# Attention with a mixture of experts on one core: row sums completed on VectorE instead of GpSimd, a batch's gating in 22 small steps further apart, another order of work within a pair of heads

## The chip, the cores and the metric

One core of a Trainium2 chip runs the kernel. The metric is the device time of one execution in microseconds. The engines are TensorE (PE in the profile; its weight loads are PEld), VectorE (DVE), ScalarE (ACT), GpSimd (POOL) and SyncE (SP), which issues most DMAs. Each takes its instructions in the order in which the program holds them.

## The reference

Attention over 8 batches, 8 heads, 576 positions and 64 numbers a head, float32, with a threshold: scores that lie more than tau under their row's maximum count as nothing. Its output is the input of a mixture of 8 experts, of which each token takes the two with the highest noisy logit.

```python
scores = scale * np.matmul(q, k.transpose(0, 1, 3, 2))
thresh = np.max(scores, axis=-1, keepdims=True) - tau
scores = np.where(scores >= thresh, scores, -1000000000.0)
attn = np.exp(scores - np.max(scores, axis=-1, keepdims=True))
attn = attn / (np.sum(attn, axis=-1, keepdims=True) + 1e-09)
x = np.matmul(attn, v)            # then (B, S, H * D) -> (4608, 512)
logits = x @ w_gate
noisy_logits = logits + np.log1p(np.exp(x @ w_noise)) * noise
top2 = np.argpartition(-noisy_logits, 2, axis=1)[:, :2]
# top2_w: softmax of the two logits; for each expert e and its tokens:
out[mask] += top2_w[mask, k, None] * (np.maximum(x[mask] @ w1[e], 0.0) @ w2[e])
```

## The kernel before

The program has two stages. In the attention stage, up to about 640 us, the work goes in 32 pairs of heads, n = 0 to 31, four for each batch, in the order of their numbers but overlapped: a pair's score work runs beside the value work of the pair before it.

For a pair, `split` cuts keys and queries into a high part (hik, hiq, on ACT, L199) and the rest (lok, loq, on POOL, L200); the scores are three products of these on PE (`scores`, L240), into two PSUM buffers sp. There are nine row blocks a pair, 0 to 8; block 0 holds the two heads' last 64 rows, 1 to 8 are 128 rows each. For each block VectorE reads sp and takes the row maximum (`rowmax`, L253, called R0 to R8 below), ACT the exponentials e (L255) and the threshold thr (L259), and VectorE masks e by the threshold into p and sums the row (`mask`, L278; M0 to M8). PE transposes p in pieces (`ptile`, L289), ACT copies them to pt (L291), and PE multiplies them with the values (`avpiece`, `avrem`, L343). `pcorner` (L315, L317) and `prem` (L304 to L308) do the same for the last 64 rows and columns. `norm` adds 1e-9 to the row sums on POOL (L328, L329), `invert` takes their reciprocals on VectorE (L334, L335); `oev` copies the product out (L370, ACT), `xlpart` transposes it and multiplies it with the gate's weights (L386, L387), `xev` scales it with the reciprocals (L400, VectorE; X0, X1).

After its fourth pair a batch is gated by ten functions, most of them on POOL, during the following three pairs: sums of the logits (t, lgs), softplus of the noise scale (ab, ge, gln, gu, gr, gc), the two largest of eight (`gate_max`), their one-hot rows (oh), ranks within each expert by a product on PE (`gate_rank`: mb, rk), slots (sl). Then ten scatters, each an indirect DMA that POOL issues (`gate_put`, L617, with a memset of a spacer ahead of it), write the tokens into slot_table, in DRAM.

In the second stage, to the end, the experts run: tokens are read from the table (ti, L809, SP; ix, L819, VectorE), gathered (L839, POOL), multiplied (L893, L914) and added to the output by indirect DMA (L935, POOL). The first expert starts on the tokens of batches 0 to 5 before the attention stage ends.

The order of work on every engine is written out by hand. Each call gets a key, and the calls are issued in the order of their keys:

```python
    for n in range(NP):
        g = 9 * n
        d = dict(PAIR, **(LAST if n == NP - 1 else {}))
...
    for _, _, f, a in sorted(ev, key=lambda x: x[:2]):
        f(*a)
```

So nine units of a key are one pair. `PAIR` holds the offsets of a pair's calls, `LAST` those of the last pair, `GATING` those of a batch's gating behind the last xev of its fourth pair, and `START` those of the first expert, counted from G = 9 x 32.

Of the kernel before, what the change touches and what calls it, by code (L numbers as in the profile page):

```python
# [27 lines left out]
NB = 5  # L28
# [15 lines left out]
    mask=(1.47, 3.69, 4.19, 5.44, 6.30, 7.74, 7.98, 8.87, 9.48),
    ptile=(3.86, 4.04, 7.93, 7.95, 10.00, 8.13, 13.46, 10.48, 12.98), pcorner=(5.79,), prem=(10.10,), norm=(14.32,),
    invert=(14.85,), avrem=(14.96,), avpiece=(11.09, 12.01, 12.31, 14.67, 15.74, 15.85, 16.05, 16.25),
    oev=(16.02, 16.72), xlpart=(16.96, 19.35, 20.02), xev=(18.74, 20.37), split_q=(-7.96,), split_k=(-9.92,))
# [3 lines left out]
    mask=(1.32, 1.83, 4.56, 2.84, 5.96, 6.40, 7.00, 9.93, 10.16),  # L51
    ptile=(4.62, 6.52, 7.86, 5.64, 10.07, 8.69, 9.18, 10.55, 10.85), pcorner=(2.03,), prem=(11.01,), norm=(10.90,),
    invert=(11.92,), avrem=(11.47,), avpiece=(11.27, 11.29, 11.64, 11.68, 11.41, 11.44, 12.80, 12.82),
    oev=(12.91, 13.26), xlpart=(13.13, 13.45, 14.05), xev=(13.15, 14.22))
# [4 lines left out]
GATING = (0, 2, 2.2, 3.5, 5, 7, 8, 10.5, 11.3, 13)  # L59
# [12 lines left out]
    gate=(6, 7, 7, 8, 8, 9, 9, 10, 11, 11), put=(12, 12, 12, 13, 13, 13, 13, 13, 13, 13), tokb=13, ixb=17,  # L72
# [71 lines left out]
def attention(tc, const, work, psum, state, qk, v, tau, wgn, noise, noise_r, out, x_dram, table, experts):  # L144
# [401 lines left out]
    def gate_max(b):  # L546
        d = gt[b]
        d["mx"] = small([NB, 8], F32, "mx")
        d["ix"] = small([NB, 8], U32, "ix")
        for i in range(NB):  # L550
            vec.max(d["mx"][:, i, :], d["nl"][:, i, :])
        for i in range(NB):
            vec.max_index(d["ix"][:, i, :], d["mx"][:, i, :], d["nl"][:, i, :])
# [640 lines left out]
```

## Time and profile before

| what | us |
|---|---|
| median of 3 runs (1490.82 to 1495.47) | 1493.9 |
| the profiled execution | 1491.48 |
| its span | 1489.7 |
| busy: PE, VectorE, ACT, POOL | 1407.6, 875.8, 699.9, 590.0 |

The profile is of one execution, whose mean granted clock of TensorE was 0.975 of full speed. An engine's busy time counts its instructions' durations; what is left of the span it waits. Since each engine goes in order, an instruction that waits holds up all that stand behind it on its engine.

### The profile page before, as it was taken

How to read it: one execution, taken by the hardware profiler on the slowest of the kernel's cores; microseconds unless marked ns; L12 is line 12 of the kernel's file. 1: busy time of each engine (PE TensorE's matmuls, PEld its weight loads, DVE VectorE, ACT ScalarE, POOL GpSimd, SP SyncE). 2: the span in 40 equal slices, each digit the busy share in tenths (PEclk: the TensorE clock that was granted, in tenths of full speed). 3: DMA queues.
4: the chain of work that ended last, by engine and by line, in shares of the span. 5: the costliest groups of instructions: out<-in, count | busy, mean ns of one | idle time of the engine just before them, and what ended most of it. 6: DMA issues, size and time to landing. Idle time of an engine off the chain costs nothing. (4 is left out here: it accounts for less than half of the span.)

```text
span 1489.7 us, 25931 instructions
## 1 busy us (share of the span) xinstructions
PE 1407.6 (94%) x9242; PEld 1200.6 (81%) x9242; DVE 875.8 (59%) x2502; ACT 699.9 (47%) x1447; POOL 590.0 (40%) x785
## 2 busy tenths in 40 slices
PE   8998989899898998898999999999999999999996
PEld 5776767677676776696998998999999999989884
DVE  7887878788787977563554354344454553543411
ACT  6996879788887876540322122122132231221210
POOL 2145454445453545553252252262352432531512
PEclk9999999999999998999999999999999999999998
DMA  5242424233332224255657466376386375563422
GB/s 169 61 132 65 132 65 132 65 111 86 99 91 61 69 60 130 72 146 114 183 125 170 105 147 150 84 160 148 91 183 150 83 183 138 123 165 92 67 28 32
DMA packets 154116, 166.32 MB, mean 112 GB/s; under 512 B 58148, under 2 KB 105340, under 8 KB 152960
## 3 DMA queue, kind: packets, MB, share of 16 engines
q1 hardware_dynamic: 126784, 125.21, 28.9%
q0 software_dynamic: 27200, 39.42, 16.0%
q8 instruction: 73, 1.20, 0.4%
q14 instruction: 59, 0.48, 0.1%
HBM read 104.42 MB, written 60.15 MB: 110 GB/s over the span
## 5 line engine op out<-in xcount | busy, mean ns | idle before, releaser
L255 ACT ACTIVATE e<-ns,nm 128x576 f32<-128x576 f32 x288 | 214.0, 772 | 90.3 <-DVE ns L253 85.9
L253 DVE TENSOR_SCALAR_CACHE_REDUCE ns<-sp 128x576 f32<-128x576 f32 x279 | 203.4, 751 | 37.2 <-PE sp L240 37.2
L278 DVE SCALAR_TENSOR_TENSOR p<-ns,thr,e 128x576 f32<-128x576 f32 x256 | 216.7, 862 | 1.2 <-ACT thr L259 1.2
L240 PE MATMUL sp<-hik,hiq 128*128 128x288 f32 (+1 forms) x558 | 124.8, 350 | 43.0 <-DVE ns L253 41.6
L289 PE MATMUL tp<-ident,p 128*128 128x128 f32 x1024 | 154.9, 289 | 8.0 <-DVE p L278 4.8
L240 PEld LDWEIGHTS sp<-hik,hiq 128*128 128x128 f32 (+1 forms) x558 | 69.5, 188 | 102.4 <-DVE ns L253 67.1
L291 ACT ACTIVATE pt<-tp 128x512 f32<-128x512 f32 x256 | 144.1, 595 | 13.4 <-PE tp L289 10.2
L343 PE MATMUL tp<-pt,vt 128*64 128x256 f32 (+1 forms) x1024 | 148.0, 414 | 0.0
L935 POOL DMA_INDIRECT out<-m_y,ix x54 | 87.8, 1627 | 150.4 <-DVE m_y L974 137.5
L935 POOL DMA_INDIRECT out<-m_y,sx x43 | 67.6, 1572 | 194.6 <-DVE m_y L916 176.0
L289 PEld LDWEIGHTS tp<-ident,p 128*128 128x128 f32 x1024 | 124.7, 152 | 17.9 <-PE tp L289 5.5
L895 ACT ACTIVATE m_p<-m_tp 128x384 fp32r<-128x384 f32 (+1 forms) x66 | 32.6, 494 | 211.8 <-PE m_tp L893 210.1
L916 DVE TENSOR_SCALAR m_y<-m_sp,gw 128x512 f32<-128x512 f32 (+1 forms) x43 | 32.3, 751 | 154.7 <-PE m_sp L914 153.3
L200 POOL TENSOR_TENSOR lok<-kq,hik 128x640 fp32r<-128x640 f32 x31 | 48.3, 1557 | 169.3 <-ACT hik L199 169.3
L240 PE MATMUL sp<-lok,hiq 128*128 128x288 f32 (+1 forms) x558 | 103.8, 301 | 0.0
L343 PEld LDWEIGHTS tp<-pt,vt 128*64 128x64 f32 x1024 | 79.7, 136 | 29.6 <-issue 10.8
L839 POOL DMA_INDIRECT m_p<-x_rows,sx x71 | 69.6, 980 | 81.6 <-DMA stage<-m_p 55.0
L240 PE MATMUL sp<-hik,loq 128*128 128x288 f32 (+1 forms) x558 | 100.3, 294 | 0.0
L617 POOL DMA_INDIRECT slot_table<-pay,sl x80 | 87.0, 1088 | 16.7 <-issue 14.1
L895 ACT ACTIVATE m_hik<-m_tp 128x384 fp32r<-128x384 f32 (+1 forms) x11 | 5.6, 506 | 181.1 <-PE m_tp L893 181.1
L893 PE MATMUL m_tp<-m_pt,m_pt 128*128 128x384 f32 (+1 forms) x396 | 73.3, 343 | 0.0
L893 PE MATMUL m_tp<-m_vt,m_pt 128*128 128x384 f32 (+1 forms) x264 | 71.8, 346 | 0.0
(349 smaller groups left out, 3504.6 us busy)
## 6 DMA issues: line engine op xcount, KB each, us to landing
m_kq<-w SPq DMA_DIRECT2D x128, 256.0 KB
kq<-qk SPq DMA_DIRECT2D x32, 640.0 KB
stage<-m_p SPq DMA_DIRECT2D x63, 256.0 KB
vt<-v SPq DMA_DIRECT2D x8, 1280.0 KB
out<-zeros SPq DMA_DIRECT2D x19, 512.0 KB
x_rows<-xr SPq DMA_DIRECT2D x32, 256.0 KB
...
```

The costliest lines, as they stand in the source:

```text
L200: nc.gpsimd.tensor_tensor(lo, x, hi.bitcast(F32), op=ALU.subtract)
L240: nc.tensor.matmul(sp[s][:, hh, 0:HALF], q_[p, 128 * t:128 * t + 128] if j else q_[:, 512:640], k_[p, k0:k0 + HALF], start=(i == 0), stop= ...
L253: nc.vector.tensor_scalar(ns, sp[:, :, 0:HALF], -1.0 / math.sqrt(D) if n else scale, None, op0=ALU.mult, op1=ALU.min, accum_out=nm)
L255: nc.scalar.activation(e, ns, AF.Exp, bias=nm, scale=-1.0)
L278: nc.vector.scalar_tensor_tensor(p, ns, thr, e, op0=ALU.is_le, op1=ALU.mult, accum_out=ssum[n][:, c:c + 1])
L289: nc.tensor.transpose(tp[:, kt, :], p[:, 128 * kt:128 * kt + 128], ident)
L291: nc.scalar.activation(pt[n][:, s, :, COLS[t]:COLS[t] + 128], tp, AF.Copy)
L343: nc.tensor.matmul(av[n, i][64 * s:64 * s + 64, 0:PIECES[i][1] - PIECES[i][0]], w, x, start=(k == 1), stop=(k == 5))
L617: st = nc.gpsimd.indirect_dma_start(out=table, out_offset=bass.IndirectOffsetOnAxis(ap=d["sl"][0:m, i, c:c + 1], axis=0), in_=d["pay"][0:m ...
L839: self.nc.gpsimd.indirect_dma_start(out=r[0:m], out_offset=None, in_=x, in_offset=bass.IndirectOffsetOnAxis(ap=self.tok[e][2][0:m, t:t + 1 ...
L893: nc.tensor.matmul(ps[:, 0:n], w[:, 128 * c:128 * c + 128], x[:, c, 0:n], start=(i == 0), stop=(i == len(ops) - 1))
L935: st = self.nc.gpsimd.indirect_dma_start(out=out, out_offset=bass.IndirectOffsetOnAxis(ap=idx, axis=0), in_=y, in_offset=None, compute_op= ...
```

## The change

`norm` becomes one addition on VectorE (L327) over the 128x9 block of row sums; the sums of the last rows of the second head, which L328 moved across partitions, are now moved by the reciprocal (L331). The ten gating functions become fourteen: the reciprocal gr, the sum of the one-hot rows and the addition of the base ranks stand by themselves, and the five maxima and the five index searches are issued one by one, at offsets up to 17.8 rather than 13. The scatters follow 18.6 units behind the last xev rather than 14.8, 0.85 apart. The offsets of `PAIR` and `LAST` are other numbers, so are some of `START`. Lines after L253 mostly move by a few: scores L241, row maximum L254, e L256, thr L260, mask L279, splits L200 and L201, scatter L624, ix L828.

```diff
 PAIR = dict(
-    scores=(-1.65, 0.71, 1.60, 3.60, 6.29), rowmax=(-0.38, 1.14, 1.15, 1.78, 1.82, 4.85, 5.21, 6.69, 7.81),
+    scores=(-1.92, -0.37, 3.30, 4.27, 5.98), rowmax=(-1.42, 1.95, 2.09, 3.33, 3.37, 5.08, 5.21, 6.30, 6.64),
...
-GATING = (0, 2, 2.2, 3.5, 5, 7, 8, 10.5, 11.3, 13)
+GATING = (0, 2.2, 2.4, 3.6, 5.2, 5.4, (7.6, 8.1, 8.6, 9.1, 9.6), (10.1, 10.6, 11.1, 11.6, 12.1), 12.7, 13.2, 14.8, 15.6, 16.6, 17.8)
...
-    raw=(-20, -20, -10), tok=-35, ix=-30, ga=(-30, -28, -26), ba=(-28, -26, -24), la=(-26, -22, -20), ta=(-12, -11, -8),
+    raw=(-20, -20, -10), tok=-31, ix=-27, ga=(-27, -25, -23), ba=(-25, -23, -21), la=(-23, -20, -18), ta=(-12, -11, -8),
...
     def norm(n):
 
-        r = ssum.pop(n)
-
-        eng = nc.vector if experts and n >= NP - 2 else nc.gpsimd
-        eng.tensor_scalar(r[0:64, 9:10], r[64:128, 8:9], 1e-9, None, op0=ALU.add)
-        eng.tensor_scalar(r[:, 0:9], r[:, 0:9], 1e-9, None, op0=ALU.add)
-        rn[n] = r
+        r = rn[n] = ssum.pop(n)
+        nc.vector.tensor_scalar(r[:, 0:9], r[:, 0:9], 1e-9, None, op0=ALU.add)
 
     def invert(n):
         r = rn[n]
+        nc.vector.reciprocal(r[0:64, 9:10], r[64:128, 8:9])
         nc.vector.reciprocal(r[:, 0:9], r[:, 0:9])
-        nc.vector.reciprocal(r[0:64, 9:10], r[0:64, 9:10])
...
+    def gate_inverse(b):
+        u, c, r = gt[b]["soft"]
+        vec.reciprocal(r, u)
+
     def gate_soft2(b):
         eng = engine(b)
         d = gt[b]
         l, (u, c, r) = d["l"], d["soft"]
-        vec.reciprocal(r, u)
         eng.tensor_tensor(c, c, r, op=ALU.mult)
...
-            x = g + d["xev"][1]
+            x = g + max(d["xev"])
...
-                to = x + 14.8 + 0.9 * i
+                to = x + 18.6 + 0.85 * i
```

The first place is POOL's row among the scatters of the first batch. Behind "waits" stand semaphores: DMASW belongs to the DMAs that POOL issues, DMAHW to the loads, and each other to an engine. Before:

```order
L616 MEMSET spacer 1x1 [waits Pool_49]
L617 DMA slot_table<-pay_1793,sl_1836 37152x2
L616 MEMSET spacer 1x1 [waits Pool_49]
L617 DMA slot_table<-pay_1793,sl_1836 37152x2
L616 MEMSET spacer 1x1 [waits Pool_49]
L617 DMA slot_table<-pay_1793,sl_1836 37152x2
L328 TENSOR_SCALAR ssum_1673<-ssum_1673 64x1 [waits DMASW4_49,DMASW3_49,DMASW5_49,DMASW2_49,DMASW6_49,DMASW1_49,DMASW0_49]
L329 TENSOR_SCALAR ssum_1673<-ssum_1673 128x9 [waits DVE_49,Pool_49]
L616 MEMSET spacer 1x1
L617 DMA slot_table<-pay_1793,sl_1836 37152x2
L616 MEMSET spacer 1x1 [waits Pool_49]
L617 DMA slot_table<-pay_1793,sl_1836 37152x2
```

Now:

```order
L624 DMA slot_table<-pay_1996,sl_2044 37152x2
L623 MEMSET spacer 1x1 [waits Pool_49]
L624 DMA slot_table<-pay_1996,sl_2044 37152x2
L623 MEMSET spacer 1x1 [waits Pool_49]
L624 DMA slot_table<-pay_1996,sl_2044 37152x2 [waits DMASW0_49]
L201 TENSOR_TENSOR lok_2260<-kq_1783,hik_2259 128x640 [waits Activation_49]
L623 MEMSET spacer 1x1 [waits Pool_49]
L624 DMA slot_table<-pay_1996,sl_2044 37152x2 [waits DMASW1_49]
L201 TENSOR_TENSOR loq_2393<-kq_2072,hiq_2392 128x640 [waits DMAHW3_49,PE_49,Activation_49]
```

L328 and L329 are gone from among the scatters; a scatter now follows the other, with lok between the ninth and the tenth.

The second place is POOL's row in a batch's first gating pair, where xr is the logits, gu, gc and gr belong to the noise scale. Before:

```order
L200 TENSOR_TENSOR loq_1354<-kq_1000,hiq_1353 128x640 [waits PE_49,Activation_49]
L501 TENSOR_TENSOR t_1423<-xr_120 128x320 [waits DVE_49]
L504 TENSOR_TENSOR t_1425<-t_1423 128x160 [waits Pool_49]
L506 TENSOR_TENSOR lgs_1427<-t_1425 128x80 [waits Pool_49]
L328 TENSOR_SCALAR ssum_1133<-ssum_1133 64x1 [waits Pool_49]
L329 TENSOR_SCALAR ssum_1133<-ssum_1133 128x9 [waits Pool_49]
L528 TENSOR_SCALAR gu_1514<-ge_1483 128x40 [waits Activation_49]
L529 TENSOR_SCALAR gc_1515<-gu_1514 128x40 [waits Pool_49]
L530 TENSOR_TENSOR gc_1515<-ge_1483,gc_1515 128x40 [waits Pool_49]
L538 TENSOR_TENSOR gc_1515<-gc_1515,gr_1516 128x40 [waits DVE_49,Pool_49]
```

Now:

```order
L498 TENSOR_TENSOR t_1483<-xr_120 128x320 [waits DVE_49]
L501 TENSOR_TENSOR t_1485<-t_1483 128x160 [waits Pool_49]
L503 TENSOR_TENSOR lgs_1487<-t_1485 128x80 [waits Pool_49]
L201 TENSOR_TENSOR loq_1562<-kq_1250,hiq_1561 128x640 [waits DMAHW7_49,PE_49,Activation_49]
L524 TENSOR_SCALAR gu_1593<-ge_1569 128x40 [waits Activation_49]
L525 TENSOR_SCALAR gc_1594<-gu_1593 128x40 [waits Pool_49]
L526 TENSOR_TENSOR gc_1594<-ge_1569,gc_1594 128x40 [waits Pool_49]
L537 TENSOR_TENSOR gc_1594<-gc_1594,gr_1595 128x40 [waits DVE_49,Pool_49]
L538 TENSOR_TENSOR gc_1594<-gc_1594,gln_1571 128x40 [waits Activation_49,Pool_49]
```

The subtraction loq, ahead of the logits' sums before, now stands between them and gu.

The third place is VectorE's row in the same pair, around the reciprocal gr; p masks of blocks M and pr the mask of block 0 (M0), ns the row maxima. Before:

```order
L334 RECIPROCAL ssum_1133<-ssum_1133 128x9 [waits Pool_49]
L335 RECIPROCAL ssum_1133<-ssum_1133 64x1
L278 SCALAR_TENSOR_TENSOR p,ssum_1381<-ns_1410,thr_1406,e_1412 128x576
L253 TENSOR_SCALAR ns_1535,nm_1536<-sp_1520 128x576 [waits DVE_49,PE_49]
L537 RECIPROCAL gr_1516<-gu_1514 128x40 [waits Pool_49]
L278 SCALAR_TENSOR_TENSOR p,ssum_1381<-ns_1477,thr_1479,e_1481 128x576 [waits Activation_49]
L253 TENSOR_SCALAR ns_1569,nm_1536<-sp_1521 128x576 [waits DVE_49,PE_49]
```

Now:

```order
L254 TENSOR_SCALAR ns_1548,nm_1549<-sp_1534 128x576 [waits DVE_49,PE_49]
L510 SCALAR_TENSOR_TENSOR ab_1567<-lgs_1487 128x40 [waits Pool_49]
L279 SCALAR_TENSOR_TENSOR p,ssum_1354<-ns_1516,thr_1518,e_1520 128x576 [waits Activation_49]
L279 SCALAR_TENSOR_TENSOR p,ssum_1354<-ns_1523,thr_1518,e_1525 128x576
L279 SCALAR_TENSOR_TENSOR p,ssum_1354<-ns_1468,thr_1462,e_1470 128x576
L531 RECIPROCAL gr_1595<-gu_1593 128x40 [waits Pool_49]
L279 SCALAR_TENSOR_TENSOR pr_1626,ssum_1625<-ns_1548,thr_1550,e_1552 128x576 [waits DVE_49,Activation_49]
L254 TENSOR_SCALAR ns_1628,nm_1629<-sp_1576 128x576 [waits DVE_49,PE_49]
```

The reciprocal gr, between a row maximum and a mask before, now follows four masks with a row maximum among them and stands just ahead of M0.

With these tables VectorE's row of a pair without gating reads, after the change: R1 R2 X0 R3 R4 M1 M2 M3 M4 R5 R6 X1, norm and the two reciprocals, R7 R8 M5, R0 of the next pair, M7 M8 M6, M0 of the next pair. On ACT hik stands between the fourth and the fifth e of a row of nine, hiq behind the copies that follow the e of block 0.

## Rows read from the trace of the kernel before

**Rows 1.** The page's part 1, busy time of each engine.
```profile
PE 1407.6 (94%) x9242; PEld 1200.6 (81%) x9242; DVE 875.8 (59%) x2502; ACT 699.9 (47%) x1447; POOL 590.0 (40%) x785
```

**Rows 2.** Windows: a pair without gating, then one batch's first three gating pairs.
```profile
57.99:74.37 16.38, 16.38 (x154) 12.54 (x154) 14.22 (x42) 15.27 (x33) 3.63 (x5) 1.00 0.30 90
...
90.76:107.91 17.15, 17.13 (x158) 13.00 (x156) 14.29 (x42) 15.60 (x35) 10.62 (x16) 1.00 0.75 216
107.91:126.56 18.65, 18.15 (x161) 13.50 (x158) 17.05 (x65) 15.65 (x34) 6.62 (x14) 1.00 0.23 65
126.56:150.79 24.23, 17.57 (x137) 13.82 (x138) 16.54 (x44) 15.24 (x32) 15.66 (x25) 0.88 0.21 50
```

**Rows 3.** Windows 90.76 to 475.91, one for each of five batches: sum line.
```profile
sum 385.15, PE 349.51 PEld 266.47 DVE 308.59 ACT 310.11 POOL 181.88; mean PE 69.90 PEld 53.29 DVE 61.72 ACT 62.02 POOL 36.38
```

**Rows 4.** Windows 475.91 to 589.39; timeline of PE, floor pair's first score matmul.
```profile
568.08:589.39 21.31, 14.24 (x126) 9.81 (x122) 12.85 (x53) 11.98 (x26) 9.56 (x16) 0.90 0.35 104
sum 113.48, PE 101.73 PEld 76.54 DVE 90.56 ACT 89.39 POOL 59.30; mean PE 16.96 PEld 12.76 DVE 15.09 ACT 14.90 POOL 9.88
...
70.95 0.40 PE L240 MATMUL sp<-hik,hiq 128*128 128x288 f32 x1
```

**Rows 5.** Waits between 100 and 600 us: total, times, longest.
```profile
DVE ssum L334 <- POOL ssum L329: 46.7, 7, 7.9
```

**Rows 6.** Timeline of POOL, VectorE and PE in the first stall.
```profile
143.54 0.23 POOL L328 TENSOR_SCALAR ssum<-ssum 64x1 f32<-64x1 f32 x1 [4.28 <-DMA slot_table<-pay,sl]
...
144.15 0.22 DVE L334 RECIPROCAL ssum<-ssum 128x9 f32<-128x9 f32 x1 [6.96 <-POOL ssum L329]
...
145.84 0.61 PE L240 MATMUL sp<-hik,hiq 128*128 128x288 f32 x1 [5.81 <-DVE ns L253]
```

**Rows 7.** Windows after the first stall.
```profile
146.00:150.00 4.00, 4.00 (x20) 3.98 (x21) 4.00 (x11) 3.42 (x8) 2.27 (x5) 0.50 0.03 3
```

**Rows 8.** Timeline: loq on POOL and what VectorE ran beside it; a mask alone.
```profile
60.53 1.61 POOL L200 TENSOR_TENSOR loq<-kq,hiq 128x640 fp32r<-128x640 f32 x1 [0.98 <-ACT hiq L199]
...
61.56 0.76 DVE L253 TENSOR_SCALAR_CACHE_REDUCE ns<-sp 128x576 f32<-128x576 f32 x1 [0.84 <-PE sp L240]
...
66.38 0.81 DVE L278 SCALAR_TENSOR_TENSOR p<-ns,thr,e 128x576 f32<-128x576 f32 x1
...
110.44 1.56 POOL L200 TENSOR_TENSOR loq<-kq,hiq 128x640 fp32r<-128x640 f32 x1 [0.98 <-ACT hiq L199]
...
110.75 1.87 DVE L278 SCALAR_TENSOR_TENSOR pr<-ns,thr,e 128x576 f32<-128x576 f32 x1
```

**Rows 9.** Groups of instructions (page, all, 100 to 600 us); tile ssum's L329.
```profile
L255 ACT ACTIVATE e<-ns,nm 128x576 f32<-128x576 f32 x288 | 214.0, 772 | 90.3 <-DVE ns L253 85.9
L253 DVE TENSOR_SCALAR_CACHE_REDUCE ns<-sp 128x576 f32<-128x576 f32 x279 | 203.4, 751 | 37.2 <-PE sp L240 37.2
L278 DVE SCALAR_TENSOR_TENSOR p<-ns,thr,e 128x576 f32<-128x576 f32 x256 | 216.7, 862 | 1.2 <-ACT thr L259 1.2
...
L291 ACT ACTIVATE pt<-tp 128x512 f32<-128x512 f32 x256 | 144.1, 595 | 13.4 <-PE tp L289 10.2
...
L259 ACT ACTIVATE thr<-nm,atau 128x2 f32<-128x2 f32 (+1 forms) x160 | 45.6, 285 | 0.0
...
L199 ACT ACTIVATE hiq<-kq,some 128x640 fp32r<-128x640 f32 x31 | 25.6, 827 | 0.0
...
L528 POOL TENSOR_SCALAR gu<-ge 128x40 f32<-128x40 f32 x7 | 3.4, 488 | 9.2 <-ACT ge L518 9.2
...
L329 DVE TENSOR_SCALAR ssum<-ssum x2: 173/509/845, 605.8 to 618.0; 128x9 f32<-128x9 f32 x2
```

**Rows 10.** Timeline: last early scatter (POOL), table read (SP), its use (VectorE).
```profile
530.04 1.10 POOL L617 DMA_INDIRECT slot_table<-pay,sl  x1 [0.21 <-issue]
...
533.79 1.72 SPq L809 DMA_DIRECT2D ti<-slot_table  x4
...
546.20 0.24 DVE L819 TENSOR_SCALAR ix<-ti,jq 128x24 int32<-128x24 int32 x1
```

More of the change, by code (lines that the diff above doesn't have):

```diff
@@ L42 @@
 PAIR = dict(
-    scores=(-1.65, 0.71, 1.60, 3.60, 6.29), rowmax=(-0.38, 1.14, 1.15, 1.78, 1.82, 4.85, 5.21, 6.69, 7.81),
[L44 to L47, printed above, removed]
-LAST = dict(
[L51 to L54, printed above, removed]
+    scores=(-1.92, -0.37, 3.30, 4.27, 5.98), rowmax=(-1.42, 1.95, 2.09, 3.33, 3.37, 5.08, 5.21, 6.30, 6.64),
+    mask=(1.85, 3.58, 4.11, 5.05, 5.06, 7.09, 9.10, 8.99, 9.05),
+    ptile=(7.22, 6.78, 10.70, 6.07, 7.59, 12.31, 12.70, 10.22, 10.71), pcorner=(5.58,), prem=(11.03,), norm=(14.52,),
+    invert=(15.23,), avrem=(13.45,), avpiece=(12.87, 13.19, 13.58, 14.04, 13.51, 14.11, 16.71, 17.48),
+    oev=(14.49, 19.23), xlpart=(19.31, 20.92, 22.57), xev=(20.54, 23.30), split_q=(-10.40,), split_k=(-5.20,))
+LAST = dict(
+    scores=(-1.92, -0.37, 2.95, 4.28, 5.25), rowmax=(-1.42, 1.77, 2.48, 2.96, 3.44, 4.42, 4.44, 6.36, 7.05),
+    mask=(1.53, 3.58, 3.71, 5.27, 6.21, 7.13, 7.68, 7.76, 9.27),
+    ptile=(5.83, 5.88, 7.88, 9.38, 9.72, 8.52, 9.17, 9.65, 10.24), pcorner=(4.70,), prem=(10.27,), norm=(11.04,),
+    invert=(11.25,), avrem=(11.10,), avpiece=(10.38, 11.53, 11.59, 11.60, 11.05, 11.37, 11.43, 11.61),
+    oev=(11.68, 12.89), xlpart=(14.08, 13.17, 13.40), xev=(14.49, 13.65))
 MLAG = 2
-GATING = (0, 2, 2.2, 3.5, 5, 7, 8, 10.5, 11.3, 13)
+GATING = (0, 2.2, 2.4, 3.6, 5.2, 5.4, (7.6, 8.1, 8.6, 9.1, 9.6), (10.1, 10.6, 11.1, 11.6, 12.1), 12.7, 13.2, 14.8, 15.6, 16.6, 17.8)
 PIECES = ((0, 320), (320, 576))
@@ L71 @@
     l1b=(6, 7, 9, 9, 11, 13, 14, 15), l2=(16, 17, 19, 23, 25, 27), eng=0, put0=(2, 2, 2, 3, 3, 3, 3, 3, 3, 4),
[L72 removed]
+    gate=(6, 7, 7, 8, 8, 8, 9, 9, 9, 9, 10, 10, 11, 11), put=(12, 12, 12, 13, 13, 13, 13, 13, 13, 13), tokb=13, ixb=17,
     gc=(17, 17, 18, 19), bc=(18, 19, 19, 20), lc=(19, 20, 20, 24), tc=(22, 23, 25, 27), tok1=-18, ix1=1,
@@ L544, in gate_soft2, with gate_max, gate_index @@
         eng.tensor_tensor(d["nl"], c, l[:, :, 0:8], op=ALU.add)
-    def gate_max(b):
+    def gate_max(b, i):
         d = gt[b]
[L548 to L553, printed above, removed]
+        if i == 0:
+            d["mx"] = small([NB, 8], F32, "mx")
+            d["ix"] = small([NB, 8], U32, "ix")
+        vec.max(d["mx"][:, i, :], d["nl"][:, i, :])
+    def gate_index(b, i):
+        d = gt[b]
+        vec.max_index(d["ix"][:, i, :], d["mx"][:, i, :], d["nl"][:, i, :])
     def gate_hot(b):
@@ L562, in gate_hot, with gate_both @@
                           f.rearrange("p k c -> p (k c)")[:, :, None].to_broadcast([128, 2 * NB, E]), op=ALU.is_equal)
-        dl = small([NB], F32, "dl")
+    def gate_both(b):
+        eng = engine(b)
+        d = gt[b]
+        dl = d["dl"] = small([NB], F32, "dl")
         eng.tensor_tensor(dl, d["mx"][:, :, 1], d["mx"][:, :, 0], op=ALU.subtract)
-        d["dl"] = dl
         o = d["oh"].rearrange("p (k c) e -> p k c e", c=2)
@@ L569, in gate_rank @@
     def gate_rank(b):
-        eng = engine(b)
         d = gt[b]
         m = mb[b % 2]
-        ps = bank("rank")[:, 0:(NB + 1) * E].rearrange("p (k e) -> p k e", e=E)
+        ps = d["ps"] = bank(("rank", b))[:, 0:(NB + 1) * E].rearrange("p (k e) -> p k e", e=E)
         nc.tensor.matmul(ps, tri, m, start=True, stop=False)
@@ L579, in gate_rank, with gate_base @@
         nc.scalar.activation(d["e2"], d["dl"], AF.Exp)
+    def gate_base(b):
+        eng = engine(b)
+        d = gt[b]
         rk = small([NB + 1, E], F32, "rk")
-        vec.tensor_tensor(rk, ps, base[:, None, :].to_broadcast([128, NB + 1, E]), op=ALU.add)
-        done("rank")
+        vec.tensor_tensor(rk, d["ps"], base[:, None, :].to_broadcast([128, NB + 1, E]), op=ALU.add)
+        done(("rank", b))
         vec.tensor_copy(base, rk[:, NB, :])
```

10 lines of the change are left out of this document (6 added, 4 removed).

## The prediction

> **What bounds the kernel now.** I read the page's busy times first: PE is busy 1407.6 us, 94% of the span, and no other engine passes 60% [rows 1]. So only PE's idle time, or PE at a low clock, can be saved. The windows cut the attention stage into pairs, from one lok subtraction on POOL to the next. A pair without gating takes 16.38 us with PE busy 16.38 at clock 1.00, DVE 14.22, ACT 15.27; this is the floor, and as the change leaves PE's instructions alone it stays the floor. The pairs that carry a batch's gating take 17.15, 18.65, 24.23 us [rows 2]. The third holds the stall: PE is busy 17.57 of 24.23, at a mean clock of 0.88. Five whole batches take 385.15 us [rows 3], where twenty floor pairs would take 20 x 16.38 = 327.6; the excess is 57.5 us, 11.5 each. The rest of the stage, from 475.91 to the first score matmul of the last pair at 589.39, is 113.48 us. Undisturbed it would be five pairs and the 12.96 us that lie between a lok and the next pair's first score matmul (57.99 to 70.95): 94.9. Its excess is 18.6 [rows 2, 4]. Together 76.0 us of the stage is not floor.
>
> Where is it? In the waits, VectorE's reciprocal L334 waits for POOL's L329 seven times, 46.7 us in all [rows 5]. The timeline of the first shows the chain: POOL's L328, which adds 1e-9 to a pair's row sums, sits idle 4.28 us for scatters into the slot table; L334 then ends an idle of 6.96 us, and PE's next score matmul one of 5.81 [rows 6]. Then PE's clock is 0.50 [rows 7], one of its two levels, half of the other. What the clock takes away is 24.23 x (1 - 0.88) = 2.9 us [rows 2]. So one stall is 5.8 + 2.9 = 8.7 us of a batch's 11.5. The rest is about the excess of the first two gating pairs, 0.77 and 2.27.
>
> **The change, part by part.** *Row sums on VectorE.* Two POOL instructions go, one VectorE add of 128x9 comes (0.17 us, as the row of L329 where VectorE ran it [rows 9]). VectorE is free 2.2 us in a floor pair [rows 2], and the add stands where it next waits for scores, so I cost it at nothing; without that cover it is 0.17 x 28 = 5 us. What matters: the order of POOL before shows L328 as the instruction that waits for all seven open scatters, and after the change nothing in POOL's row takes over that wait: lok and loq wait only for ScalarE, PE and the loads, and the ninth and tenth scatters wait for the first and second, long landed. So the stall goes: seven times 8.7 us, of which the last clock loss lies past 589.39 and is not in the 76.0. To be shared out are thus 76.0 + 2.9 = 78.9 us.
>
> *New order in a pair.* The same operations in another order. The sum of PE's work is unchanged. ACT with 15.27 and VectorE with 14.22 + 0.17 stay below 16.38, so a pair can still close at the floor; the longest loop that I find through rowmax, e, thr, mask and back comes to some 16.3, so I allow 0.1 us a pair for waits that don't fit: 2.8 us in 28 pairs; bounds 0 and 0.3 x 28 = 8.
>
> *lok and loq beside masks.* This is where the order could cost. At 110.44 loq ran 1.56 us on POOL, and the mask that VectorE started at 110.75 took 1.87 us, where one alone takes 0.81 (66.38); the row maximum at 61.56, started beside a loq of 1.61, took 0.76, the mean being 0.75 [rows 8, 9]. So a mask that starts after a split waits for it. In the new row loq becomes ready behind R7 by one R, two e, thr, two pt, e, thr, pt and hiq: 0.75 + 1.54 + 0.29 + 1.20 + 0.77 + 0.29 + 0.60 + 0.83 = 6.3 us by full durations [rows 9], some 5.7 as neighbours overlap; the mask M0 of the remainder, behind R7 R8 M5 R0 M7 M8 M6, starts after 3 x 0.75 + 4 x 0.81 = 5.5, overlapped about 5.0. M0 is first by 0.7 us. For lok against M4 the same count gives 0.3 us. After either mask VectorE has 2 to 4 us of work with at most one operand from SBUF. So in plain pairs I cost the splits at nothing; bounds 0 and 1.06 us for each of two masks a pair. The Trainium skill ("SBUF — State Buffer", section "Who interferes with whom") says that the port pair that VectorE and GpSimd share is an exclusive lock, that a VectorE instruction with two SBUF inputs contends with a GpSimd one that reads SBUF, and that one with at most one does not; the mask and the row maximum above agree, with 1.87 and 0.76 us.
>
> *Gating spread out, and what POOL now holds behind the splits.* POOL's order puts loq ahead of gu in the first pair, and VectorE's row has the reciprocal gr, which needs gu, between M6 and M0. By the counts above VectorE is at gr at 5.2 us behind R7; loq ends at 5.7 + 1.6 = 7.3 and gu 0.49 later [rows 9]: a wait of 2.5 us, with M0 and the next row maxima queued behind it and PE behind those. In the second pair mb comes behind loq in the same way; PE's rank matmuls wait for it, and with them the transposes and scores behind: 1.2 to 1.7 us. In the third, small steps: 0.2. In the fourth lok stands behind nine scatters of 1.1 us, each with its spacer [rows 10], and comes about 1.3 us late for the next scores. Sum 5.2 to 5.7; I take 5.5 a batch, against 11.5. The 5.8 us stall brought half clock; PE's new gaps are 2.5 us at most. No row among these shows a gap of that size, so I add a quarter of 2.9 us, 0.7: 6.2. The lower bound is nothing (all of it in slack), the upper 5.5 + 2.9 = 8.4.
>
> *Later scatters against earlier tokens.* Before, the last early scatter began at 530.04, the token table was read at 533.79 and VectorE's ix used it at 546.20, 16.2 us after that scatter [rows 10]. In the tables the step from last scatter to ix shrinks from 8.65 units to 5.4, a unit being 16.38 / 9 = 1.82 us: 9.8 us. The read follows its scatter by 3.75 us, takes 1.7 to issue [rows 10] and must land. If the scatter also runs late, ix waits, and in VectorE's row M0 and the row maxima stand behind it. Once; bounds 0 and 7 us plus 2.9 of clock; I take 3. The expert stage, PE-bound, is otherwise the same code; its order shift I put at 0, within 5 us either way.
>
> **Sum.** Excess after: six gatings x 6.2 = 37.2, the seventh's first pairs before the last pair 4, fit 2.8, ix 3: 47.0. Saved 78.9 - 47.0 = 31.9. The profiled execution took 1491.5 us, 2.4 under the median of the runs shown; 1491.5 - 31.9 = 1459.6, on the median's scale **1462 us**.
>
> **Rivals.** *(a) The waits are smaller.* If the new waits mostly fall into the 2.2 us that VectorE has free in each pair, a gating costs 3: 18 + 2 + 2.8 = 23, saved 56, **1438 us**. For it: all are counted by a chain whose slack I know to some 0.5 us. Against: gu, behind a whole loq, is in the printed order.
>
> *(b) The stall only moves.* PE's 2.5 us gap halves the clock in each gating, and ix waits fully: 6 x 8.4 + 5 + 2.8 + 9.9 = 68, saved 11, **1483 us**. For it: the clock did fall at 5.8 us. Against: PE has transposes and value matmuls to do for part of the wait.
>
> *(c) Slower: the splits take the port first.* If VectorE runs 0.7 us later in its row than counted (0.3 for M4), lok and loq start ahead of M4 and M0, and both masks grow by 1.87 - 0.81 = 1.06 us in each of 28 pairs [rows 8], with the scores behind: 59 us, so 1462 + 59 = **1521 us**; with only one of them 1492. For it: the margins are thin, and a delay once made keeps the order. Against: a late VectorE also makes e, and so hiq and hik, late, so the margin holds unless VectorE waits for PE in between.
>
> *(d) It doesn't remove the wait.* Another POOL instruction could meet the open scatters, or the VectorE add the POOL writes. The order shows none; time as before, **1494 us**.
>
> **How the numbers follow.** Chances: forecast 0.50 (its own range 1450 to 1474), (a) 0.20, (b) 0.12, (c) 0.13, (d) 0.05. The range for 8 in 10 takes in (a) and (b), with a few us for the expert stage: 1434 to 1488; (c) and (d) are left out. A difference under 0.3%, 4.5 us, can hardly be told from none. Faster by more: the forecast, (a) and most of (b), 0.81. Within: (d) and the half of (c) with one mask, 0.09. Slower: 0.10.
>
> **What would show it.** Right: no POOL instruction waits for the slot table in the stage; L332's wait is for nothing; plain pairs of 16.4 to 16.6 us at clock 1.00; VectorE idle about 2.5 us at L531 in each batch's first gating pair; a wait at L588 or of PE for mb in the second; batches of 70 to 73 us rather than 77. Wrong: plain pairs of 17 us or more, masks of 1.5 us and more beside L201 (rival c); clock 0.5 in every batch (b); no idle at L531 (a).

## The result, and the profile after

The changed kernel took 1470.1 us (median; 1468.8 to 1473.3), the one before 1492.4 in the same comparison: a ratio of 0.9857 (95% interval 0.9823 to 0.9891), 22 us faster. The forecast was 1462 within 1434 to 1488. The profiled execution took 1471.25 us with a span of 1469.5: 20.2 less than the 1491.48 of before, where the sum had 31.9.

The page's busy times of the changed kernel:

```profile
PE 1410.2 (96%) x9242; PEld 1189.8 (81%) x9242; DVE 884.9 (60%) x2530; ACT 695.2 (47%) x1447; POOL 555.4 (38%) x725
```

Against [rows 1] PE has the same 9242 instructions and 2.6 us more busy time, in a span that is 20.2 us shorter: its idle time fell from 82.1 to 59.3 us. So the gain is waiting that PE no longer does, and a little of it is given back in the work itself. Where, the windows tell. Here they run from the first score matmul of a pair's block 0 to that of the next pair; those of [rows 2] were cut at lok, somewhat earlier. A pair without gating, a batch's first four gating pairs, and the next batch's first (the columns: length; busy time of PE, PEld, DVE, ACT, POOL; granted clock; DMA share, GB/s):

```profile
58.06:74.78 16.72, 16.72 (x153) 12.52 (x151) 14.59 (x43) 15.10 (x33) 3.36 (x2) 1.00 0.15 39
108.30:128.73 20.43, 18.68 (x153) 14.05 (x151) 15.37 (x50) 15.64 (x35) 6.51 (x12) 0.92 0.67 185
128.73:147.39 18.66, 17.46 (x158) 12.90 (x157) 17.36 (x59) 15.30 (x34) 6.33 (x13) 1.00 0.21 58
147.39:164.11 16.72, 16.72 (x152) 12.52 (x150) 14.59 (x43) 15.09 (x33) 12.22 (x19) 1.00 0.18 60
164.11:181.12 17.01, 16.91 (x153) 12.55 (x151) 14.59 (x43) 15.22 (x33) 6.79 (x8) 1.00 0.36 86
181.12:200.07 18.95, 17.20 (x153) 12.71 (x151) 15.37 (x50) 15.64 (x35) 6.52 (x12) 1.00 0.69 193
```

By the same cut the first batch's third gating pair and the pair behind it were, before:

```profile
122.56:145.84 23.28, 16.62 (x152) 12.55 (x151) 15.89 (x42) 14.95 (x32) 13.22 (x20) 0.98 0.21 52
145.84:164.90 19.06, 19.06 (x150) 15.02 (x151) 15.22 (x44) 16.46 (x34) 6.07 (x9) 0.85 0.20 64
```

So the wait lay in the third and most of the half clock in the fourth; now both are about plain pairs. The first grew instead, to 20.43 or 18.95 according to the clock, and a plain pair takes 16.72 where it took 16.38. The six stretches of four pairs from 91.50 to 527.28 us average (527.28 - 91.50) / 6 = 72.6 us, against 385.15 / 5 = 77.0 [rows 3].

The waits between 100 and 600 us say which engine waits for which line (total, times, longest). In place of the 46.7 us of [rows 5] there are two new ones, and none for the slot table:

```profile
DVE gr L531 <- POOL gu L524: 15.9, 7, 2.3
```

The other, PE's matmuls L577 for mb (POOL, L571), is 6.7 us in seven. The timeline of POOL and VectorE in the first gating pair shows how the first of them arises (start, duration, instruction; in brackets the idle time ahead of it and what ended it):

```profile
113.28 1.54 POOL L201 TENSOR_TENSOR loq<-kq,hiq 128x640 fp32r<-128x640 f32 x1 [4.69 <-ACT hiq L200]
114.79 0.34 POOL L524 TENSOR_SCALAR gu<-ge 128x40 f32<-128x40 f32 x1
115.17 0.40 DVE L531 RECIPROCAL gr<-gu 128x40 f32<-128x40 f32 x1 [2.28 <-POOL gu L524]
115.49 0.72 DVE L279 SCALAR_TENSOR_TENSOR pr<-ns,thr,e 128x576 f32<-128x576 f32 x1
```

POOL had been idle for 4.69 us, but loq stands ahead of gu in its order. VectorE stands at gr for 2.28 us, and M0 (pr) and the row maxima come behind that; PE's next scores end an idle of 1.18 us. In the second pair:

```profile
133.70 1.55 POOL L201 TENSOR_TENSOR loq<-kq,hiq 128x640 fp32r<-128x640 f32 x1 [8.09 <-ACT hiq L200]
133.86 1.49 DVE L562 TENSOR_TENSOR oh<-iota,gf 128x80 f32<-128x80 f32 x1
135.43 0.78 POOL L571 TENSOR_TENSOR mb<-oh 128x40 bf16<-128x40 f32 x1
136.25 0.18 PE L577 MATMUL tp<-mb,tri 128*128 128x48 bf16 x1 [1.00 <-POOL mb L571]
```

The one-hot rows oh, an instruction with two inputs from SBUF, start 0.16 us behind loq, and take 1.49 us, to the end of loq; mb and PE's rank products come behind it. The groups of tile oh, here of after (eight times, least, median and longest ns), then of before:

```profile
L562 DVE TENSOR_TENSOR oh<-iota,gf x8: 242/1484/1492, 133.9 to 632.2; 128x80 f32<-128x80 f32 x8
```

```profile
L561 DVE TENSOR_TENSOR oh<-iota,gf x8: 241/243/244, 112.7 to 654.9; 128x80 f32<-128x80 f32 x8
```

So six times as long, in six of the eight batches, for an instruction that the new order puts beside a split.

### The profile page after: what moved, and what is told of

It reads as the page before. It is cut to its first block, busy times and chain, and to the rows that moved or that the text cites. A ratio compares the mean times of both kernels' runs of the same rounds, so it can differ in the third digit from the quotient of the medians.

```text
span 1469.5 us, 25882 instructions
## 1 busy us (share of the span) xinstructions
PE 1410.2 (96%) x9242; PEld 1189.8 (81%) x9242; DVE 884.9 (60%) x2530; ACT 695.2 (47%) x1447; POOL 555.4 (38%) x725
## 3 DMA queue, kind: packets, MB, share of 16 engines
q0 software_dynamic: 27200, 39.42, 16.4%
## 5 line engine op out<-in xcount | busy, mean ns | idle before, releaser
L256 ACT ACTIVATE e<-ns,nm 128x576 f32<-128x576 f32 x288 | 213.1, 771 | 72.6 <-DVE ns L254 64.1
L254 DVE TENSOR_SCALAR_CACHE_REDUCE ns<-sp 128x576 f32<-128x576 f32 x279 | 201.4, 753 | 48.1 <-PE sp L241 45.2
L279 DVE SCALAR_TENSOR_TENSOR p<-ns,thr,e 128x576 f32<-128x576 f32 x256 | 202.3, 828 | 12.1 <-ACT thr L260 11.6
L292 ACT ACTIVATE pt<-tp 128x512 f32<-128x512 f32 x256 | 149.5, 593 | 25.0 <-PE tp L290 23.3
L340 PE MATMUL tp<-pt,vt 128*64 128x256 f32 (+1 forms) x1024 | 159.8, 427 | 0.0
L290 PEld LDWEIGHTS tp<-ident,p 128*128 128x128 f32 x1024 | 118.0, 148 | 27.9 <-issue 10.5
L241 PE MATMUL sp<-hik,hiq 128*128 128x288 f32 (+1 forms) x558 | 117.8, 347 | 14.9 <-DVE ns L254 14.8
L201 POOL TENSOR_TENSOR loq<-kq,hiq 128x640 fp32r<-128x640 f32 x31 | 49.8, 1606 | 169.1 <-ACT hiq L200 165.3
L241 PEld LDWEIGHTS sp<-hik,hiq 128*128 128x128 f32 (+1 forms) x558 | 64.6, 186 | 55.0 <-DVE ns L254 20.7
L241 PE MATMUL sp<-lok,hiq 128*128 128x288 f32 (+1 forms) x558 | 99.4, 299 | 0.2
L201 POOL TENSOR_TENSOR lok<-kq,hik 128x640 fp32r<-128x640 f32 x31 | 52.5, 1692 | 123.6 <-ACT hik L200 123.5
L241 PE MATMUL sp<-hik,loq 128*128 128x288 f32 (+1 forms) x558 | 97.3, 295 | 0.0
L624 POOL DMA_INDIRECT slot_table<-pay,sl x80 | 82.0, 1025 | 17.6 <-issue 14.0
```

The source lines that it names most:

```text
L201: nc.gpsimd.tensor_tensor(lo, x, hi.bitcast(F32), op=ALU.subtract)
L241: nc.tensor.matmul(sp[s][:, hh, 0:HALF], q_[p, 128 * t:128 * t + 128] if j else q_[:, 512:640], k_[p, k0:k0 + HALF], start=(i == 0), stop= ...
L254: nc.vector.tensor_scalar(ns, sp[:, :, 0:HALF], -1.0 / math.sqrt(D) if n else scale, None, op0=ALU.mult, op1=ALU.min, accum_out=nm)
L256: nc.scalar.activation(e, ns, AF.Exp, bias=nm, scale=-1.0)
L279: nc.vector.scalar_tensor_tensor(p, ns, thr, e, op0=ALU.is_le, op1=ALU.mult, accum_out=ssum[n][:, c:c + 1])
L290: nc.tensor.transpose(tp[:, kt, :], p[:, 128 * kt:128 * kt + 128], ident)
```

## Experiments

The kernel before was run again in each comparison, and took 1485.4 us in that of the first four kernels, 1489.2 in that of the next four and 1495.8 in that of the last four; each ratio is to the one of its own comparison. The first four ran on another chip than the other eight. All kernels compute the whole reference.

**e1: the row sums on VectorE, everything else as before.** Is it the wait or the order that pays?

```diff
-        eng.tensor_scalar(r[0:64, 9:10], r[64:128, 8:9], 1e-9, None, op0=ALU.add)
-        eng.tensor_scalar(r[:, 0:9], r[:, 0:9], 1e-9, None, op0=ALU.add)
-        rn[n] = r
+        r = rn[n] = ssum.pop(n)
+        nc.vector.tensor_scalar(r[:, 0:9], r[:, 0:9], 1e-9, None, op0=ALU.add)
...
+        nc.vector.reciprocal(r[0:64, 9:10], r[64:128, 8:9])
         nc.vector.reciprocal(r[:, 0:9], r[:, 0:9])
-        nc.vector.reciprocal(r[0:64, 9:10], r[0:64, 9:10])
```

> The kernel before with one part of the change alone: the addition of 1e-9 and both reciprocals on VectorE, every table of the order as before. Theory A (the wait of POOL's addition for the open scatters, with the half clock behind it, was nearly the whole excess, and the new order costs on its own): the stall of 8.7 us goes from seven batches and some 3.3 us a batch stay, so about 1492 - 57 = 1435 us, plain pairs at 16.4 us, batches at 68 to 70 us; faster than the change itself by some 35 us. Theory B (with the old tables the wait only moves: lok stands behind all ten scatters on POOL, so the scores wait there): batches at 73 us or more, 1465 us or more.

1442.8 us, ratio 0.971 (0.9692 to 0.9727): 42.6 us faster than before. Windows, a plain pair and the first three gating pairs, which together are a batch:

```profile
71.55:87.94 16.39, 16.39 (x152) 12.54 (x150) 14.46 (x43) 15.24 (x33) 3.16 (x2) 1.00 0.25 73
87.94:104.75 16.81, 16.79 (x152) 12.74 (x151) 13.89 (x43) 15.12 (x34) 7.67 (x8) 1.00 0.60 170
104.75:123.49 18.74, 18.04 (x159) 13.39 (x157) 17.22 (x65) 15.43 (x34) 8.14 (x17) 1.00 0.38 110
123.49:140.96 17.47, 16.61 (x153) 12.62 (x151) 16.99 (x45) 15.84 (x34) 11.73 (x18) 1.00 0.28 70
```

The third pair is 23.28 - 17.47 = 5.8 us shorter than before, and the pair behind it is a plain one of 16.39. The four take 69.4 instead of 77.0. The run as a whole gained less than the 57 us that had been expected, but that edit alone gives the whole gain and more; the new tables cost. The addition itself is hidden, as the plain pair of 16.39 shows.

**e2: the reverse, the changed kernel with the row sums on GpSimd.** The diff is e1's backwards, on the changed kernel.

> The changed kernel with this one part undone: the additions on POOL again, in two instructions, and the old reciprocals, every table as after the change. In POOL's row the addition then stands behind the tenth scatter and waits for all that are open. Theory A: the stall is back in seven batches, 5.8 us of PE idle and 2.9 us of clock each, about 1470 + 60 = 1530 us, with VectorE's reciprocal waiting some 7 us seven times. Theory B (the new order had already moved the row sums away from the scatters): 1470 to 1480 us.

1532.9 us, ratio 1.0311 (1.0291 to 1.0332), 47 us slower than before. The stall is back, and the first one longer than in [rows 6]; VectorE's timeline:

```profile
172.96 0.22 DVE L335 RECIPROCAL ssum<-ssum 128x9 f32<-128x9 f32 x1 [10.62 <-POOL ssum L330]
```

So the wait belongs to POOL's additions among the scatters. The new tables alone cost 47 us with them, and 21 us without: the changed kernel would take 1464.2 there by the ratio 0.9857 (an estimate: it was not run in that comparison), against e1's 1442.8.

**e3: gr behind X0, so that it no longer stands at a gu behind loq.**

```diff
-GATING = (0, 2.2, 2.4, 3.6, 5.2, 5.4, ...
+GATING = (0, 2.2, 2.4, 3.6, 6.0, 6.1, ...
```

> The changed kernel with the reciprocal gr and what follows it at offsets 6.0 and 6.1 in place of 5.2 and 5.4: in VectorE's row gr then stands behind M0, two row maxima and X0 of the next pair, about 2.4 us later. Theory A (VectorE's wait of 2.27 us for gu behind loq is paid by PE in full, and in four of seven batches by the clock too): the first gating pair falls from 18.95 or 20.5 us to some 17.0, together 7 x 2.2 + 4 x 1.6 = 22 us, 1448 us. Rival: the wait moves to the first maximum, since POOL's chain behind gr takes 3.2 us: less than half of that, 1460 us or more.

1449.0 us, ratio 0.9747 (0.9729 to 0.9765), some 15 us under the estimate of 1464.2. The first gating pair:

```profile
106.61:123.73 17.12, 16.82 (x153) 12.52 (x151) 15.45 (x50) 15.54 (x35) 6.29 (x12) 1.00 0.76 207
```

17.12 us at full clock, where it took 20.43 or 18.95: all but 0.4 of the first pair's excess is that wait and the clock behind it.

**e4: mb on VectorE**, behind oh, rather than on POOL.

```diff
-        eng.tensor_tensor(mb[b % 2][:, 0:NB, :], o[:, :, 0, :], o[:, :, 1, :], op=ALU.add)
+        vec.tensor_tensor(mb[b % 2][:, 0:NB, :], o[:, :, 0, :], o[:, :, 1, :], op=ALU.add)
```

> The changed kernel with the sum of the one-hot rows, mb, on VectorE in place of POOL, where it stood behind loq. Theory A (PE's wait of 1.00 us for mb in each second gating pair is paid in full): 18.66 falls to about 17.7 us in seven pairs, 7 us in all, 1463 us. Rival: VectorE, with 17.36 us busy in that pair, is what bounds it, and an instruction of some 0.2 us more on it makes it no shorter: 1470 to 1472 us.

1481.0 us, ratio 0.9963 (0.995 to 0.9976): 17 us slower than the estimate for the changed kernel, which neither theory had. VectorE's timeline, then the second pair:

```profile
134.01 1.49 DVE L562 TENSOR_TENSOR oh<-iota,gf 128x80 f32<-128x80 f32 x1
135.54 0.20 DVE L571 TENSOR_TENSOR mb<-oh 128x40 bf16<-128x40 f32 x1
135.65 0.81 DVE L279 SCALAR_TENSOR_TENSOR pr<-ns,thr,e 128x576 f32<-128x576 f32 x1
```

```profile
128.88:149.04 20.16, 18.99 (x158) 14.07 (x156) 17.56 (x60) 15.41 (x34) 6.09 (x13) 0.92 0.23 67
```

mb takes 0.20 us and PE's longest wait for it falls from 1.0 to 0.4 us, but oh still takes 1.49 beside loq, and mb now stands ahead of M0 and the row maxima. Five of six second pairs ran at a clock of 0.92, some 1.5 us longer; the one at full clock is no shorter than the 18.66 of the changed kernel:

```profile
427.57:446.48 18.91, 17.55 (x159) 12.86 (x157) 17.57 (x60) 15.32 (x34) 5.93 (x13) 1.00 0.16 44
```

So moving mb without oh gains nothing. Of the 17 us, 3 x 1.6 + 3 x 1.5 = 9.3 are the clock, and not all of that is the edit's: the first gating pairs ran at 0.92 all seven times rather than four, though the edit lies behind them, and five second pairs rather than two.

**e5: e3, and oh away from loq** (the searches closer together, oh and what follows 2.3 units later).

```diff
-(7.6, 8.1, 8.6, 9.1, 9.6), (10.1, 10.6, 11.1, 11.6, 12.1), 12.7, 13.2, 14.8, 15.6, 16.6, 17.8)
+(7.6, 8.1, 8.4, 8.7, 9.0), (9.2, 9.4, 9.6, 10.1, 10.6), 15.0, 15.05, 15.75, 16.0, 16.6, 17.8)
```

> The changed kernel with gr behind X0 as in the run e3, and beside it the one-hot comparison oh behind X0 too (offsets 15.0, 15.05, 15.75, 16.0 for hot, both, rank and base), the index searches earlier. In the changed kernel oh, an instruction with two SBUF inputs, stands just ahead of M0 and takes 1.49 us beside loq, 0.24 where it ran before the change. Theory A (in the second gating pair oh waits for the port that loq holds, and everything behind it on VectorE waits too): the second pair falls from 18.66 to 17.0 us or less, seven times, and the whole lies some 0.8% under the run e3. Rival (PE's wait for mb behind loq is the cause, as the prediction has it): mb still stands behind loq, the pair stays above 18.2 us.

1460.2 us, ratio 0.9804 (0.9781 to 0.9828). The second pair went from 18.66 to:

```profile
124.10:141.66 17.56, 16.89 (x159) 12.66 (x157) 15.67 (x53) 15.20 (x34) 6.95 (x14) 1.00 0.29 83
```

So 1.1 of the 1.94 us that the second pair lost are gone with the collision of oh and loq (oh takes 0.24 us there); 17.0 us or less had been expected, and what holds the other 0.84 is open. e5 moves mb along with oh, so it doesn't separate the two; e4, which moved mb alone, says that oh had to go. But in ratio to before, e5 is behind e3, since the pair with the scatters took 18.1 to 20.9 us, with a wait of VectorE that e1 to e4 had not shown (c1, below).

**e6: the last partial sum of a pair (xlpart) ahead of value matmuls.** Theory A was that the ends of runs of matmuls of one kind cost the plain pair its 0.34 us.

```diff
-    oev=(14.49, 19.23), xlpart=(19.31, 20.92, 22.57), ...
+    oev=(14.49, 19.23), xlpart=(19.31, 20.92, 22.44), ...
```

> The changed kernel with one number of the order other: the third logits product (XL2) at 22.44 instead of 22.57, so that on PE it stands ahead of the remainder's value matmuls rather than between two runs of value matmuls. Theory A (the plain pair lost 0.34 us since each end of a run of value matmuls costs PE's next weight load 0.38 to 0.49 us, and the new order has five such ends where the old had four): 16.72 falls to 16.4 us, 8 us or more in 29 pairs. Rival (the new order's loop over VectorE and ACT sets 16.72): no change.

1484.5 us, ratio 0.9961 (0.9943 to 0.9979). A plain pair takes 16.69 instead of 16.72, where A had 16.4: A falls.

**e7: the first pair's first mask later**, for the 1.36 us gap of PE at 12 us.

```diff
+        if n == 0:
+            d["mask"] = (2.2,) + d["mask"][1:]
```

> The changed kernel with the mask M0 of the very first pair behind its R1 and R2 (offset 2.2 for 1.85 in that pair alone). In the changed kernel M0 waits there 1.03 us for thr with R1 and R2 behind it, PE idles 1.36 us, and its clock is 0.50 from 12 to 25 us. Theory A (that one wait costs the head its clock): PE's gap at 10.7 falls under 0.6 us, the clock stays at 1.00, the second pair's first score matmul comes at about 22 us rather than 25.4, 3 us in all. Rival (the head is bound by VectorE's masks and by lok): within 1 us of 25.4.

1484.3 us, ratio 0.9961 (0.9941 to 0.9982). The gap shrank to 0.45 us, but the clock from 12 to 16 us was still 0.56. The second pair's scores began at 22.96 us rather than 25.44; that this is the edit's doing isn't shown, since the unaltered program has them at 23.47 in c1 (below) and c2, with the edit, at 23.52.

**e8: e5, e6 and e7 together.**

> The edits of e5, e6 and e7 together on the changed kernel. If their causes are apart, the gains add: 15 us of gr, 12 of oh, 8 of XL2 and 3 of the head, so about 38 us under the changed kernel, a ratio of about 0.960 to the kernel before, and under the kernel before with VectorE's row sums (0.971). If the plain pair is bound by a loop once a wait is gone, 20 us or less: 0.972 or more.

1458.8 us, ratio 0.98 (0.9776 to 0.9824), which is e5's within the intervals, and not the 0.960 of gains that add.

e6 and e7 lay nearer to before than the changed kernel in its own comparison, though they take only fractions of a microsecond away. So the changed kernel was run again, ten times, with e7's and e5's edits beside it.

**c1: the changed kernel, unaltered.**

> The changed kernel itself once more. The runs e5 to e8 hold a wait of VectorE of 2.4 us ahead of the row maximum R5 in the pair with the scatters, which the profile of the changed kernel and the runs e1 to e4 do not hold, though its program is but for one instruction that of e7. Theory A (that wait comes and goes with the chip or the execution): it is seen here too or not, but c1, c2 and c3 have it alike. Theory B (it comes with those edits): c1 is at a ratio of 0.986 with scatter pairs of 16.7 us, c2 and c3 have it.

1492.3 us, ratio 0.9976 (0.9957 to 0.9995): on this chip the same program gains 0.24%. Its plain pairs are still 16.72 us; the six pairs with scatters take 21.79, 21.03 and four times about 18.9 instead of 16.72 to 17.1. VectorE's and PE's timeline in the first, and the pair:

```profile
161.42 0.76 DVE L254 TENSOR_SCALAR_CACHE_REDUCE ns<-sp 128x576 f32<-128x576 f32 x1 [3.90 <-PE tp L316]
```

```profile
159.24 0.38 PE L340 MATMUL tp<-pt,vt 128*64 128x256 f32 x1 [0.24 <-issue]
159.95 0.64 PE L340 MATMUL tp<-pt,vt 128*64 128x256 f32 x2 [0.34 <-issue]
```

```profile
144.49:166.28 21.79, 19.52 (x153) 13.91 (x151) 15.61 (x45) 15.34 (x33) 13.59 (x21) 0.91 0.31 76
```

VectorE does nothing for 3.90 us ahead of the row maximum R5, while the scatters run; the releaser that the view infers, a transpose on PE, is no input of R5. PE's value matmuls pause in the same stretch, twice, for nothing that the profile shows ("issue"). From the second pair's first scores to the last pair's it is 563.2 us here and 542.9 in the first profile of the same program: 20 us more, most of it in the pairs with scatters.

**c2: e7 again.**

> The program of e7 once more, beside the changed kernel. Theory A: 2 to 3 us under c1, the head alone, with the same scatter pairs as c1. Theory B: about 1% over c1, as e7 stood to the changed kernel, with the wait ahead of R5.

1489.9 us, ratio 0.9967 (0.9951 to 0.9983): 2.4 us under c1, with intervals that overlap. The same wait ahead of R5, and the same start: the second pair's first score matmul in c1, then in c2:

```profile
23.47 0.59 PE L241 MATMUL sp<-hik,hiq 128*128 128x288 f32 x1
```

```profile
23.52 0.38 PE L241 MATMUL sp<-hik,hiq 128*128 128x288 f32 x1
```

So the first pair's gap of 1.36 us, which c1 has and c2 doesn't, costs the start nothing there.

**c3: e5 again.**

> The program of e5 once more, beside the changed kernel. Theory A: under c1 by the wait for gr (15 us) and by 1.1 us in seven second pairs (8 us), so 20 us or more, whether or not the wait ahead of R5 is there. Theory B: less than 10 us under c1.

1464.5 us, ratio 0.9799 (0.9762 to 0.9836): 27.8 us under c1, beside which it ran, where 20 or more had been expected. The two waits that the new gating table makes cost that much there.

**e9: e1, with the gating of before a little further apart** (the additions of base ranks behind the next mask, M0 clear of loq), for the version that beats both.

```diff
-GATING = (0, 2, 2.2, 3.5, 5, 7, 8, 10.5, 11.3, 13)
+GATING = (0, 2, 2.2, 3.5, 5, 7.85, 8.25, 10.5, 11.25, 11.3, 13)
...
+    def gate_base(b):
...
-        vec.tensor_tensor(rk, ps, base[:, None, :].to_broadcast([128, NB + 1, E]), op=ALU.add)
+        vec.tensor_tensor(rk, d["ps"], base[:, None, :].to_broadcast([128, NB + 1, E]), op=ALU.add)
```

> The kernel before with VectorE's row sums (e1), and in its gating the maxima, index searches and one-hot rows behind the mask M0 rather than ahead of it, and the addition of the base ranks a step later. In e1 the second gating pair takes 18.74 us: M0 takes 1.85 us beside loq, and VectorE waits 1.39 us for the ranks. If both waits are paid by PE, the pair falls to 17 us and the whole by 7 x 1.7 = 12 us under e1, a ratio of 0.963 to the kernel before. If VectorE's work (17.2 us in that pair) bounds it, the pair stays above 18 us and the ratio at 0.971.

1459.3 us, ratio 0.9764 (0.9728 to 0.9801), 33 us under c1 and the best of that comparison. The second pair, 18.74 in e1:

```profile
104.02:121.35 17.33, 17.04 (x159) 12.92 (x157) 16.56 (x65) 15.32 (x34) 7.36 (x17) 1.00 0.36 103
```

The pair with scatters took 20.0 to 20.4 here, with a wait like that of c1. In e9's order it stands ahead of the next pair's R0, not of R5, and ACT's copy ot stops in the same stretch:

```profile
142.83 0.39 ACT L366 ACTIVATE ot<-tp 128x256 f32<-128x256 f32 x1 [3.17 <-remote]
142.91 0.76 DVE L253 TENSOR_SCALAR_CACHE_REDUCE ns<-sp 128x576 f32<-128x576 f32 x1 [2.29 <-remote]
```

e1 was not run on this chip, nor e9 on the other, so which of them is the better stays open.

## Why the prediction was right, and where its sum was off

The mechanism was right; that the number was too is in part luck. c1, the same program, took 1492.3 us, outside 1434 to 1488, largely by a wait for which the prediction has no term.

**The stall: right.** e1 and e2 show it from both sides. Rival (d) is out. The size, 8.7 us of wait and clock, came in the first batch: e1's third pair is 5.8 us shorter and the one behind it 19.06 - 16.39 = 2.7, where 5.8 and 2.9 were counted. On average e1's batches are 77.0 - 69.4 = 7.6 us shorter. The addition costs nothing in a plain pair, since it runs while VectorE has to wait for scores anyway:

```profile
73.00 0.15 DVE L327 TENSOR_SCALAR ssum<-ssum 128x9 f32<-128x9 f32 x1
73.19 0.16 DVE L331 RECIPROCAL ssum<-ssum 64x1 f32<-64x1 f32 x1
73.38 0.21 DVE L332 RECIPROCAL ssum<-ssum 128x9 f32<-128x9 f32 x1
73.96 0.76 DVE L254 TENSOR_SCALAR_CACHE_REDUCE ns<-sp 128x576 f32<-128x576 f32 x1 [0.36 <-PE sp L241]
```

Its 0.17 us was the lesser of the two in its row, 173 and 845 ns [rows 9]; the other was a sign of what the last section shows.

**The gating pairs: right in sum, partly wrong in kind.** For gr 2.5 us were forecast; 2.28 came, and e3 shows what hangs on it. For the second pair 1.2 to 1.7 us were forecast, by mb behind loq, and 18.66 - 16.72 = 1.94 came. But the step that named mb was incomplete: oh itself was held by loq first, and e4 shows that moving mb alone gains nothing. It is rival (c)'s mechanism at a place where the prediction did not look; it counted masks only. The third and fourth pairs cost 0.2 and 0.1 us instead of 0.2 and 1.3. The clock fell to 0.92 in three of the six first gating pairs that lie ahead of 527 us and in two of the second ones, 1.6 and 1.5 us each: 7.8 / 6 = 1.3 a batch against 0.7. In all 2.2 + 1.9 + 0.2 + 0.1 + 1.3 = 5.7 us a batch against 6.2.

**Rival (c): not in plain pairs.** M0 was clear of loq every time. The groups of tile pr give 719, 811 and 819 ns (least, median, longest) after, where the longest of e1, in the old order, is 1856:

```profile
L279 DVE SCALAR_TENSOR_TENSOR pr<-ns,thr,e x32: 719/811/819, 10.5 to 576.5; 128x576 f32<-128x576 f32 x32
```

```profile
L278 DVE SCALAR_TENSOR_TENSOR pr<-ns,thr,e x32: 805/815/1856, 10.8 to 550.0; 128x576 f32<-128x576 f32 x32
```

Before, M0 was held like that in seven second gating pairs (1.85 to 1.87 us, the first in [rows 8]). The new tables freed it and put oh in its place, and the second pair stayed as long: 18.74 in e1, 18.66 after.

**The fit of a pair: the term that was mis-sized.** 0.1 us was allowed, with bounds of 0 and 0.3; 16.72 - 16.38 = 0.34 came, outside the 16.4 to 16.6 us a pair that were to show the forecast right. It is the new order of a pair and not the added instruction, since e1 keeps 16.39. The profile shows no wait either: PE is busy 16.72 of 16.72, with the same matmuls. (Their ends are modelled, so a short wait inside a run of them would not show.) So the step failed by which the floor stays at 16.38 because PE's instructions stay the same; the 0.1 was allowed for waits, and PE's busy time grew. Where, the starts in PE's timeline tell, if each run of matmuls of one kind is counted up to the start of the next kind. The scores take 4.87 us in a plain pair of e1 and of the changed kernel alike, the value matmuls 5.04 and 5.21, the partial sums 0.66 and 0.75, the transposes of p 5.09 and 5.16. In e6 the value matmuls are back at 5.03 and the partial sums take 0.88: its edit moved the cost on to another kind. That the order of the kinds makes it is thus likely; by which neighbours is open.

**Where the 11.7 us went** by which 20.2 falls short of 31.9. Three stretches hold them all. *The start, 4.3, not in the sum:* the second pair's first scores come at 25.44 instead of 21.13 us. PE idles 1.36 us for the first row maxima, and its mean clock from 12 to 24 us is 0.50, where before had 0.86:

```profile
12.10 3.02 PE L241 MATMUL sp<-kq 64*128 64x288 f32 x8 [1.36 <-DVE ns L254]
```

That this gap costs the 4.3 us isn't shown. c2, without it, starts no earlier than c1, with it, and c1 has 2 of the 4.3 back, at a clock of 0.51.

*From there to the last pair's first scores, 3.7:* the sum had 47.0 us of excess over floor pairs. The fit took 30 x 0.34 = 10.2 instead of 2.8, 7.4 more; the gatings of six batches took 34.5 instead of 37.2; the two pairs from 527.28 on, the seventh's first among them, took 20.60 + 20.50 - 2 x 16.72 = 7.7, at a clock of 0.92, instead of the 4 and the 3 that were put down to the seventh's first pairs and ix, though ix itself waited for no token. That is 7.4 - 2.7 + 0.7 = 5.4. Against it stand the first four pairs, 0.8 under four of 16.72, and the excess before, which counted from its second pair is 76.9 rather than 76.0 us. *The tail, 3.7:* 901.1 us from the last pair's scores to the end against 900.3, where the sum expected the last of the clock losses, 2.9, to be saved.

**What stays open.** VectorE's wait in the pairs with scatters. All eight kernels on that chip have such a wait, c1 and e9 too (e9 ahead of R0); the first profile of the changed kernel, whose chip is not on record, and e1 to e4, on the other chip, do not. PE or ACT can stop with VectorE, as c1 and e9 show. Nothing that was found in the traces explains it. Before has its stall in that place, which would cover it; that was only argued. So the size of this change's gain, 1.4% or 0.2%, depends on something that these runs don't settle, while e5's gating table kept its 2% against before in two comparisons on the chip that shows the wait.
